# Splitting the weights in the first woven period of a delta-rule attention and MLP kernel: the remainder on VectorE, loads on other queues, the last unit woven in

## The chip, the cores and the metric

The kernel runs on one core of one Trainium2 chip. The metric is the device time of one execution in microseconds; for the kernel before it is the median of three runs. Where a single execution is taken apart, it is the profiled one, with its own time.

## The reference

q, k and v have 4 batches, 8 heads, 768 steps and 48 elements a head, in float32. Each head carries a 48 x 48 state; step by step the output is the state read with q, and the state is then corrected by the delta rule:

```python
k_n = k / (np.linalg.norm(k, axis=-1, keepdims=True) + 1e-06)
for t in range(S):
    y[:, :, t] = np.einsum('bhd,bhde->bhe', q[:, :, t], state)
    v_old = np.einsum('bhde,bhd->bhe', state, kt)
    state = state + bt[:, :, :, None] * np.einsum('bhd,bhe->bhde', kt, vt - v_old)
h = np.maximum(x @ w_in, 0.0)        # x: y as 3072 tokens x 384
return (h * h @ w_out).astype(np.float32)
```

w_in is 384 x 2048 and w_out 2048 x 384, both float64.

## The kernel before, in words

The work is cut into 12 units: two batches and 128 steps each, in two chunks of 64 steps. For a unit the kernel normalizes the keys (`normalize`), forms the products of keys with keys and queries (`static`), inverts a triangular matrix of every 32 steps by substitution on VectorE (`invert`, two instructions a step, L386 to L389), completes the inverse of 64 steps on TensorE (`whole`), carries the state through the two chunks (`sequential`) and runs the two MLP layers on its 256 tokens (`moe`). TensorE takes every float32 operand of the MLP as a high and a low half in fp32r and sums three products (L534, L547).

The weights come as float64. `fetch` loads them as pairs of 32-bit words on SP's queue in 28 pieces (three of w_in with 512 columns, then four of w_out with 384, and so on). `split_weights` turns each piece into its halves: an absolute value on ScalarE (L142), a maximum on GpSimd (L143, `least`), four instructions on VectorE that put the float32 together and form the rest below it (L150 to L157, `words`), the cast to the high half on ScalarE (L160), and on TensorE identity x float32, minus identity x high half and identity x rest, summed in PSUM and copied by ScalarE as the low half (L166, L167, `low`). The high half is written to the place from which the words were read.

The order on TensorE, VectorE, ScalarE and SP is that in which the program emits the instructions; GpSimd's is not written by hand. First come the loads of units 0 and 1 and a fixed sequence with seven pieces (0 to 6), then the inversion of units 0 and 1 together, then pieces 7 to 17 beside unit 0's state. From unit 1 on, `weave` mixes the steps of several generators: each has a number of steps and a stretch of the period, and the steps are sorted by their place. The last generator (the MLP of the unit before) is the filler: between two steps of other generators that are not marked "quiet" one of its steps is put. Pieces 18 to 27 stand in the period of unit 1, as 11 steps.

```python
        for u in range(1, units):
            parts = [(splits, NS, 0, 0.88, "")] if u == 1 else []
            ...
            parts.append((before, n_moe - OVER, M0, M1, ""))
            weave(*parts)
        take(before)
        take(moe(ds_[units - 1]))
```

## Time and profile before

| what | value |
|---|---|
| median of 3 runs | 703.48 us (701.7 to 704.35) |
| profiled execution, its own time | 702.14 us |
| its span, first to last instruction | 700.2 us |
| TensorE busy | 631.6 us, 90% |
| VectorE busy | 429.3 us, 61% |
| ScalarE busy | 332.2 us, 47% |
| GpSimd busy | 85.0 us, 12% |
| mean granted TensorE clock | 0.976 of full speed |

PE is TensorE's matmul, PEld its weight loads, DVE VectorE, ACT ScalarE, POOL GpSimd, SP SyncE. A timeline row gives start, duration, engine, line, operation, output<-input, the count, and in brackets the idle time of the engine before it with what ended it. A busy share over the whole span is an average over stages with different limits: here an opening in which TensorE has little to do, and eleven woven periods in which it has little rest.

### The profile page before, as it was taken

How to read it: one execution, taken by the hardware profiler on the slowest of the kernel's cores; microseconds unless marked ns; L12 is line 12 of the kernel's file. 1: busy time of each engine (PE TensorE's matmuls, PEld its weight loads, DVE VectorE, ACT ScalarE, POOL GpSimd, SP SyncE). 2: the span in 40 equal slices, each digit the busy share in tenths (PEclk: the TensorE clock that was granted, in tenths of full speed). 3: DMA queues.
4: the chain of work that ended last, by engine and by line, in shares of the span. 5: the costliest groups of instructions: out<-in, count | busy, mean ns of one | idle time of the engine just before them, and what ended most of it. 6: DMA issues, size and time to landing. Idle time of an engine off the chain costs nothing.

```text
span 700.2 us, 23645 instructions
## 1 busy us (share of the span) xinstructions
PE 631.6 (90%) x10104; PEld 579.8 (83%) x10104; DVE 429.3 (61%) x1165; ACT 332.2 (47%) x632; POOL 85.0 (12%) x110
## 2 busy tenths in 40 slices
PE   2740598798999999999999999999999999999996
PEld 1420257687999999999999999999999999999996
DVE  3599985568549468477576485593775775641221
ACT  3550366464553553544545535445545445355352
POOL 7970341210100100101001001001000010000000
PEclk9985799999999999999999999999999999999999
DMA  8788331400341441531522423415315324030100
GB/s 171 178 234 335 74 51 17 93 9 2 54 101 25 80 88 19 107 65 28 102 51 43 98 40 54 102 24 107 70 18 103 60 35 98 3 61 3 24 1 23
DMA packets 172969, 49.96 MB, mean 71 GB/s; under 512 B 164513, under 2 KB 167617, under 8 KB 172865
## 3 DMA queue, kind: packets, MB, share of 16 engines
q1 hardware_dynamic: 169920, 47.65, 32.3%
q8 instruction: 79, 1.29, 0.8%
q0 software_dynamic: 768, 0.41, 0.3%
q10 hardware_dynamic: 2176, 0.39, 0.3%
q14 instruction: 26, 0.20, 0.1%
HBM read 37.32 MB, written 11.01 MB: 69 GB/s over the span
## 4 chain that ended last, share of the span: by engine, by line
PE 80%; DVE 9%; DMA 3%; ACT 2%; issue 2%; SPq 2%; POOL 1%; DVEq 0%; ACTq 0%
PE h L547 30%; PE o L534 29%; PE g L478 3%; PE g L454 3%; PE x L447 2%; DVE tt L389 2%; PE x L300 2%; PE x L491 2%; DVE h_h L386 2%; DMA w<-in_moe_w_in_dram 1%; PE g L499 1%; PE x L166 1%; PE g L300 1%; SPq L205 1%; PE x L290 1%
## 5 line engine op out<-in xcount | busy, mean ns | idle before, releaser
L534 PE MATMUL o<-w,h_h 128*128 128x384 f32 x768 | 203.7, 346 | 0.0
L547 PE MATMUL h<-x_h,w 128*128 128x256 f32 x1152 | 172.4, 285 | 2.3 <-ACT x_h L516 1.3
L547 PEld LDWEIGHTS h<-x_h,w 128*128 128x128 f32 x1152 | 152.6, 188 | 8.0 <-ACT x_h L516 2.7
L526 DVE TENSOR_TENSOR h_l<-r,h_h 128x512 fp32r<-128x512 f32 x96 | 66.5, 692 | 147.6 <-PE o L534 59.3
L554 ACT ACTIVATE r<-h 128x512 f32<-128x512 f32 x96 | 57.4, 598 | 172.9 <-PE h L547 172.5
L534 PEld LDWEIGHTS o<-w,h_h 128*128 128x128 f32 x768 | 133.5, 189 | 2.5
L534 PE MATMUL o<-w,h_l 128*128 128x384 f32 x384 | 130.0, 338 | 0.0
L388 DVE SCALAR_TENSOR_TENSOR tmp<-lt,bt,z 128x126 f32<-128x126 f32 (+22 forms) x310 | 95.5, 308 | 21.4 <-DMA out_dram<-a 10.4
L547 PE MATMUL h<-x_l,w 128*128 128x256 f32 x576 | 99.2, 281 | 0.0
L389 DVE TENSOR_TENSOR z<-z,tmp 128x126 f32<-128x126 f32 (+22 forms) x310 | 79.2, 255 | 10.6
L547 PEld LDWEIGHTS h<-x_l,w 128*128 128x128 f32 x576 | 81.4, 188 | 0.0
L534 PEld LDWEIGHTS o<-w,h_l 128*128 128x128 f32 x384 | 72.3, 188 | 0.0
L555 ACT ACTIVATE r<-r 128x512 f32<-128x512 f32 x96 | 60.7, 632 | 3.1
L557 ACT CAST h_h<-r 128x512 fp32r<-128x512 f32 x96 | 59.5, 620 | 3.0
L372 POOL MEMSET z<- 128x512 f32 x10 | 5.5, 553 | 395.7 <-DMA inv<-z 348.8
L166 PE MATMUL o<-r,plus 128*128 128x512 f32 (+1 forms) x16 | 8.8, 637 | 28.3 <-DVE r L153 28.3
L247 DVE TENSOR_REDUCE n<-rest 128x8 f32<-128x384 f32 x22 | 11.9, 549 | 35.3 <-ACT rest L246 35.3
L143 POOL TENSOR_SCALAR a<-a 128x384 f32<-128x384 f32 (+1 forms) x18 | 24.1, 1340 | 50.4 <-ACT a L142 42.5
L439 ACT ACTIVATE tt<-x 32x256 f32<-32x256 f32 x42 | 15.7, 375 | 26.6 <-PE x L435 26.1
L166 PEld LDWEIGHTS o<-r,plus 128*128 128x128 f32 x16 | 2.7, 204 | 29.2 <-ACT s L249 28.1
L478 PEld LDWEIGHTS g<-state,kq 48*64 48x64 f32 x1408 | 22.5, 134 | 4.3 <-issue 2.8
L516 ACT CAST x_h<-h 128x384 fp32r<-128x384 f32 x24 | 11.4, 480 | 30.7 <-PE h L514 30.7
(144 smaller groups left out, 801.6 us busy)
## 6 DMA issues: line engine op xcount, KB each, us to landing
w<-in_moe_w_in_dram SPq DMA_DIRECT2D x12, 512.0 KB
w<-in_moe_w_out_dram SPq DMA_DIRECT2D x16, 384.0 KB
lt<-blocks SPq DMA_DIRECT2D x22, 256.0 KB
vt<-in_v_dram SPq DMA_DIRECT2D x96, 48.0 KB
out_dram<-a SPq DMA_DIRECT2D x48, 96.0 KB
kpad<-in_k_dram SPq DMA_DIRECT2D x88, 48.0 KB
qpad<-in_q_dram SPq DMA_DIRECT2D x84, 48.0 KB
blocks<-ap SPq DMA_DIRECT2D x48, 64.0 KB
```

What stands on the lines that cost most here:

```text
L143: nc.gpsimd.tensor_scalar(out=a.bitcast(F32), in0=a.bitcast(F32), scalar1=LEAST, scalar2=None, op0=ALU.max)
L300: nc.tensor.matmul(ps[j][b * C:(b + 1) * C, p], lhsT=kq[rows, c, p, b, 0], rhs=kq[rows, c, p, b, first:first + n].rearrange("p x t -> p (x ...
L388: nc.vector.scalar_tensor_tensor(out=tmp, scalar=bt[:, s:s + 1], op0=ALU.mult, op1=ALU.mult, **factors)
L389: nc.vector.tensor_tensor(out=z[:, :nj, s + 1:], in0=z[:, :nj, s + 1:], in1=tmp, op=ALU.subtract)
L454: nc.tensor.matmul(g[rows, c, h], lhsT=tt[rows, c, h], rhs=vt[rows, c, h], start=True, stop=True)
L478: nc.tensor.matmul(dst[to * C:(to + 1) * C, j, p], lhsT=kq[rows, c, p, b, x], rhs=s[rows, b, p], start=(x == 0 and p == 0), stop=False, sk ...
L526: nc.vector.tensor_tensor(out=h_l, in0=r, in1=h_h.bitcast(F32), op=ALU.subtract)
L534: nc.tensor.matmul(o[i], lhsT=a[:, e, i * P:(i + 1) * P], rhs=halves["wo", ft][w], start=(ft == 0 and n == 0), stop=(ft == FT - 1 and n == 2))
L547: nc.tensor.matmul(hp[:, e], lhsT=halves["wi", (kt, ft // EACH)][w][:, f], rhs=x[:, kt], start=(n == 0), stop=(n == 3 * KT - 1))
L554: nc.scalar.activation(out=r, in_=hp, func=AF.Relu)
L555: nc.scalar.activation(out=r, in_=r, func=AF.Square)
L557: nc.scalar.copy(out=h_h, in_=r)
```

## The change

High half and remainder: `words` no longer casts; a new step `high` does. In the opening the order stays as it was. In the woven period (`split_early` false) a piece takes three steps instead of one: the remainder of the piece before and the words of this one; the absolute value and maximum of the next; the low half of the piece before and the cast of this one. The remainder float32 - high half is a VectorE subtraction there, and TensorE sums two products, identity x remainder and identity x rest, instead of three. The pieces' steps become quiet ones, 35 by number.

Loads: GpSimd's queue keeps the beta of unit 0 alone; unit 0's q and unit 1's beta go to SP, unit 1's q to SP and later, after the triangles' transfers; two weight loads go ahead of unit 1's keys.

Last unit: the first two steps of its MLP are woven between the last four of the unit before, and two of its four stores are issued by ScalarE.

```diff
@@ -129,7 +129,7 @@
                 raws.append(raw)
 
     def room(x, n):
-        pool, first, second = rooms[x % 2 if x < AHEAD else 0]
+        pool, first, second = rooms[x % 2 if x < AHEAD - 1 else 0]
         return pool.tile([P, PC], I32, name=first)[:, :n], pool.tile([P, PC], I32, name=second)[:, :n]
 
     def split_weights():
@@ -156,33 +156,60 @@
             nc.vector.tensor_scalar(out=w1, in0=a, scalar1=-0x800000, scalar2=None, op0=ALU.bitwise_and)
             nc.vector.scalar_tensor_tensor(out=rest.bitcast(F32R), in0=raw[:, :, 0].bitcast(U32), scalar=2.0 ** -52,
                                            in1=w1.bitcast(F32), op0=ALU.mult, op1=ALU.mult)
-            hl = wpool.tile([P, 2, raw.shape[1]], F32R, name=place[x])
+            return x, a, rest
+
+        def high(x, a, rest):
+            hl = wpool.tile([P, 2, raws[x].shape[1]], F32R, name=place[x])
             nc.scalar.copy(out=hl[:, 0], in_=a.bitcast(F32))
             return x, a, rest, hl
 
-        def low(x, a, rest, hl, bank):
-            ps = bank()[:, :hl.shape[2]]
-            for n, (m, y) in enumerate(((ident, a.bitcast(F32)), (minus, hl[:, 0]), (plus, rest.bitcast(F32R)))):
-                nc.tensor.matmul(ps, lhsT=m, rhs=y, start=(n == 0), stop=(n == 2))
+        def low(x, a, rest, hl, formed=False):
+            ps = split_bank()[:, :hl.shape[2]]
+            first = [(plus, hl[:, 1])] if formed else [(ident, a.bitcast(F32)), (minus, hl[:, 0])]
+            for m, y in first:
+                nc.tensor.matmul(ps, lhsT=m, rhs=y, start=(m is first[0][0]), stop=False)
+            nc.tensor.matmul(ps, lhsT=plus, rhs=rest.bitcast(F32R), start=False, stop=True)
             nc.scalar.copy(out=hl[:, 1], in_=ps)
             halves[weight_parts[x][:2]] = hl[:, 0], hl[:, 1]
 
-        before, ready = None, []
-        for x in range(NW):
+        def remainder(x, a, rest, hl):
+
+            nc.vector.tensor_tensor(out=hl[:, 1], in0=a.bitcast(F32), in1=hl[:, 0].bitcast(F32), op=ALU.subtract)
+
+        before, ready, x = None, [], 0
+        while split_early:
 
             far = 3 if x < AHEAD - 3 else 1
-            while x + len(ready) < min(NW, x + far):
+            while len(ready) < far:
                 ready.append(least(x + len(ready)))
             if x == 0:
                 yield
+            now = high(*words(*ready.pop(0)))
+            if before:
+                low(*before)
+            before = now
+            x += 1
+            while len(ready) < (far if x < AHEAD - 3 else 1):
+                ready.append(least(x + len(ready)))
+            yield
+
+        low(*before)
+        before = None
+        for x in range(x, NW):
+            if before:
+                remainder(*before)
             now = words(*ready.pop(0))
+            yield
+            if not ready and x + 1 < NW:
+                ready.append(least(x + 1))
+            yield
             if before:
-                low(*before, split_bank)
-            before = now
-            while x + 1 + len(ready) < min(NW, x + 1 + (far if x + 1 < AHEAD - 3 else 1)):
-                ready.append(least(x + 1 + len(ready)))
-            yield
-        low(*before, split_bank)
+                low(*before, formed=True)
+            before = high(*now)
+            yield
+        remainder(*before)
+        yield
+        low(*before, formed=True)
         yield
 
     def split_bank():
@@ -214,7 +241,7 @@
     def load_q(d):
 
         d["qp"] = kpad[2] if d["u"] == 1 else qp
-        load_to(d["qp"], q, d, D, (nc.sync, nc.gpsimd) if d["u"] <= 1 else None)
+        load_to(d["qp"], q, d, D)
 
     def load_beta(d):
 
@@ -223,7 +250,7 @@
         t0, b0, x = d["t0"], d["b0"], C * (d["u"] == 1)
 
         by = beta[b0:b0 + 2, :, t0:t0 + P].rearrange("b h (c n s) -> b n c h s", n=2, s=HB)
-        queue = nc.gpsimd if first else nc.sync
+        queue = nc.gpsimd if d["u"] == 0 else nc.sync
         for n in range(4):
             for j in range(2):
                 queue.dma_start(out=d["bt"][x + n * H2 + j:x + (n + 1) * H2:2], in_=by[n // 2 ^ j, n % 2][:, j::2])
@@ -241,7 +268,7 @@
         for c in range(NC):
             h = slice(c * H, (c + 1) * H)
 
-            sq = (apool.tile([P, H, D], F32, name="r", bufs=2) if d["u"] == 2 else
+            sq = (apool.tile([P, H, D], F32, name="r", bufs=2) if d["u"] in (2, 3) else
                   spool.tile([P, PC], F32, name="rest")[:, :H * D].rearrange("p (h e) -> p h e", h=H))
             nc.scalar.activation(out=sq, in_=kn[:, h], func=AF.Square)
             nc.vector.tensor_reduce(out=n2[:, h], in_=sq, axis=AX.X, op=ALU.add)
@@ -284,7 +311,7 @@
 
         def transposed(c, which, bank=None):
 
-            src = (d["kp"], d["qp"])[which]
+            src = d["qp" if which else "kp"]
             tp = (x_tile(u) if bank is None else bank).rearrange("p (n t) -> p n t", n=NP)
             for p in range(NP):
                 nc.tensor.transpose(tp[:, p], src[:, c, 2 * p:2 * p + 2].rearrange("p a b -> p (a b)"), ident)
@@ -563,7 +590,7 @@
                 yield from second(fp - 2)
         for fp in (FT // 2 - 2, FT // 2 - 1):
             yield from second(fp)
-        results = []
+        results, last = [], d["u"] == units - 1
         for c in range(2):
             results.append(spool.tile([P, PC], F32, name="a")[:, :DM])
             (nc.vector.tensor_copy if c else nc.scalar.copy)(out=results[c], in_=o[c])
@@ -571,7 +598,8 @@
         for c in range(2):
             for b in range(2):
                 row = (d["b0"] + b) * S + d["t0"] + c * C
-                nc.sync.dma_start(out=out[row:row + C], in_=results[c][b * C:(b + 1) * C])
+                queue = nc.scalar if last and c == 0 else nc.sync
+                queue.dma_start(out=out[row:row + C], in_=results[c][b * C:(b + 1) * C])
 
     def take(gen, n=None):
         while n is None or n > 0:
@@ -622,7 +650,7 @@
         yield from sequential(d)
 
     F0, F1, F2 = 3, 3, 6
-    NS = NW + 1 - (1 + 6 + 4 + 7)
+    NS = 3 * (NW + 1 - (1 + 6 + 4 + 7)) + 2
     OVER, M0, M1, E2 = 3, 0.032, 0.97, 0.13
     L1, N1 = (0.22, 0.42), (0.62, 0.92)
     A1, Q1 = (0.0, 0.22), (0.34, 0.98)
@@ -634,13 +662,14 @@
     splits = split_weights()
     engines = {mybir.EngineType.PE, mybir.EngineType.SP, mybir.EngineType.DVE, mybir.EngineType.Activation}
     with tc.manual_schedule(engines=engines):
-        ds_ += [load(0), load(1)]
-        fetch(F0)
+        ds_.append(load(0))
+        fetch(F0 - 1)
+        ds_.append(load(1))
+        fetch(1)
+        load_beta(ds_[0])
         load_q(ds_[0])
-        load_q(ds_[1])
+        load_beta(ds_[1])
         fetch(F1)
-        load_beta(ds_[0])
-        load_beta(ds_[1])
         take(normalize(ds_[0]))
         take(normalize(ds_[1]))
         take(splits, 1)
@@ -652,8 +681,10 @@
         fetch(1)
         for d in pair:
             take(d, 1)
+        fetch(2)
+        load_q(ds_[1])
+        fetch(F2 - 2)
         load_v(ds_[0])
-        fetch(F2)
         take(splits, 1)
         for d in pair:
 
@@ -681,7 +712,7 @@
         before = inverse = None
         n_i = round((1 - I0) / (I1 - I0) * NI)
         for u in range(1, units):
-            parts = [(splits, NS, 0, 0.88, "")] if u == 1 else []
+            parts = [(splits, NS, 0, 0.88, "quiet")] if u == 1 else []
             if inverse:
                 parts.append((inverse, NI - n_i, 0, I1 - 1, "quiet"))
             getting = loads(u)
@@ -697,8 +728,11 @@
                 parts.append((inverse, n_i, I0, 1, "quiet"))
             parts.append((before, n_moe - OVER, M0, M1, ""))
             weave(*parts)
+
+        final = moe(ds_[units - 1])
+        weave((before, OVER + 1, 0.2, 1, ""), (final, 2, 0, 0.5, ""))
         take(before)
-        take(moe(ds_[units - 1]))
+        take(final)
 
 
 # ---- launch: one core; inputs and outputs as the reference has them ----
```

## Rows read from the trace of the kernel before

**Rows 1.** Chain of waits, 0 to 110 us: start, duration, what.

```profile
22.51 1.49 POOL a L143
...
45.60 1.22 DVE lt L379
```

**Rows 2.** Timeline of GpSimd (POOL), 0 to 190 us.

```profile
4.73 2.70 POOL L205 DMA_DIRECT2D qpad<-in_q_dram  x4
...
17.44 4.99 POOL L229 DMA_DIRECT2D bt<-in_beta_dram  x9 [0.32 <-DMA kpad<-in_q_dram]
```

**Rows 3.** Timeline of ScalarE (ACT), 0 to 190 us.

```profile
10.38 0.52 ACT L246 ACTIVATE rest<-kpad 128x384 f32<-128x384 f32 x1 [0.60 <-DMA kpad<-in_k_dram]
...
13.43 0.66 ACT L142 ACTIVATE a<-w 128x512 f32<-128x512 f32 x1 [1.30 <-DMA w<-in_moe_w_in_dram]
...
18.18 0.66 ACT L142 ACTIVATE a<-w 128x512 f32<-128x512 f32 x1 [1.86 <-DMA w<-in_moe_w_in_dram]
...
23.79 0.38 ACT L333 COPY ap<-x 128x256 f32<-128x256 f32 x1
```

**Rows 4.** Timeline of VectorE (DVE), two stretches, 5 to 185 us.

```profile
24.02 0.84 DVE L150 TENSOR_SCALAR a<-a 128x512 int32<-128x512 int32 x1 [9.38 <-POOL a L143]
...
30.12 1.49 DVE L150 TENSOR_SCALAR a<-a 128x512 int32<-128x512 int32 x1
...
111.55 0.35 DVE L150 TENSOR_SCALAR r<-r 128x384 int32<-128x384 int32 x1
...
112.93 0.56 DVE L157 SCALAR_TENSOR_TENSOR h_l<-w 128x384 fp32r<-128x384 uint32 x1
...
129.25 0.43 DVE L150 TENSOR_SCALAR a<-a 128x512 int32<-128x512 int32 x1 [2.59 <-issue]
...
164.06 0.35 DVE L150 TENSOR_SCALAR a<-a 128x384 int32<-128x384 int32 x1
```

**Rows 5.** Timeline of SP's queue, 0 to 190 us.

```profile
11.95 6.83 SPq L205 DMA_DIRECT2D kpad<-in_q_dram  x4
...
18.82 1.55 SPq L128 DMA_DIRECT2D w<-in_moe_w_out_dram  x3
...
98.79 5.42 SPq L229 DMA_DIRECT2D bt<-in_beta_dram  x8
```

**Rows 6.** Waits of SP's queue, 30 to 62 us: total, times, longest.

```profile
SPq L395 <- DVE tt L391: 12.6, 1, 12.6
```

**Rows 7.** Busy time by engine in one stretch: length, engines, PEclk, DMA share, GB/s.

```profile
111.10:178.57 67.47, 60.78 (x808) 52.56 (x809) 46.65 (x124) 34.68 (x69) 10.28 (x8) 0.97 0.16 31
```

**Rows 8.** Waits of all engines, 104 to 182 us: total, times, longest.

```profile
ACT w L160 <- DVE rest L157: 19.7, 7, 4.5
```

**Rows 9.** TensorE's busy time with line 166 alone, same stretch.

```profile
111.10:178.57 67.47, 14.85 (x40) 0.97 0.16 31
```

**Rows 10.** Timeline of TensorE (PE), 104 to 184 us.

```profile
121.69 0.81 PE L166 MATMUL x<-a,plus 128*128 128x384 f32 x2
...
122.68 0.51 PE L534 MATMUL o<-w,h_h 128*128 128x384 f32 x2
...
140.23 2.01 PE L166 MATMUL x<-a,plus 128*128 128x512 f32 x2 [2.66 <-ACT w L167]
```

**Rows 11.** Groups of VectorE by line, 111.1 to 178.57 us: busy us, mean ns, idle.

```profile
L388 DVE SCALAR_TENSOR_TENSOR tmp<-lt,bt,z 128x126 f32<-128x126 f32 (+21 forms) x29 | 9.0, 311 | 0.6
...
L389 DVE TENSOR_TENSOR z<-z,tmp 128x126 f32<-128x126 f32 (+21 forms) x29 | 7.5, 260 | 1.0
...
L526 DVE TENSOR_TENSOR h_l<-r,h_h 128x512 fp32r<-128x512 f32 x8 | 5.7, 708 | 4.7 <-ACT h_h L557 3.4 <-PE o L534 1.3
```

**Rows 12.** Timeline of all engines, 640 to 702 us.

```profile
658.99 0.82 PE L514 MATMUL h<-plus,y 128*128 128x128 f32 x6
...
660.73 0.94 PE L547 MATMUL h<-x_h,w 128*128 128x256 f32 x6 [0.93 <-DVE x_l L517]
...
694.95 2.39 SPq L574 DMA_DIRECT2D out_dram<-a  x4
```


## The prediction

> **What bounds the kernel now.** I read the page first, then the chain of waits, the timelines of single engines up to 180 us, and the waits and busy times of the first woven period. From about 180 us to the end the chain is TensorE work without gaps, so that part moves only where the change touches its last unit. The time that can move lies before.
>
> *Opening.* The chain goes through GpSimd's first maximum (L143) at 22.51 us and then VectorE to 45.60 us, where the serial inversion of units 0 and 1 (L379 on) begins [rows 1]. The maximum was not late for data: ScalarE had its input ready at 13.43 + 0.66 = 14.09 [rows 3]. GpSimd was still issuing loads, q from 4.73 and beta until 17.44 + 4.99 = 22.43 [rows 2]. So VectorE sat idle for 9.38 us before its first piece at 24.02, and seven pieces of weights then took until 45.60, 3.08 us each [rows 1, 4].
>
> *First woven period (unit 0's MLP with pieces 18 to 27 of the weights).* From its first product at 111.10 to that of the next unit at 178.57 it lasts 67.47 us; TensorE is busy for 60.78 and so idle for 6.69, VectorE is busy for 46.65 [rows 7]. ScalarE stood 19.7 us waiting for VectorE's last word instruction of a piece (L157) [rows 8]: its cast of the high half is next in its queue, and the absolute value of the next piece, which GpSimd's maximum and VectorE's words need, stands behind that cast. The pieces thus run in a ring through three engines: words of piece 22 at 129.25, of piece 27 at 164.06, so 34.81 / 5 = 6.96 us a piece [rows 4], though a piece's words alone take 112.93 + 0.56 - 111.55 = 1.94.
>
> **The change, part by part.**
>
> *Loads off GpSimd.* It loses eight q and eight beta loads and keeps the eight of unit 0's beta. Four loads took 2.70 before the waits began, so eight take 5.4, and it is free at about 4.7 + 5.4 = 10.1 instead of 22.43 [rows 2]. The next gate is ScalarE. Two weight loads now stand ahead of unit 1's keys on SP, at 1.55 / 3 = 0.52 each [rows 5]: the keys land 1.0 us later if only the issue counts, 3 if the transfer ahead counts too. I take 1.5, so the last square of unit 1 starts at 11.9 instead of 10.38. The first absolute value followed it by 13.43 - 10.38 = 3.05, 1.30 of that waiting for weights, which now come sooner: 11.9 + 1.75 = 13.6. Three of 0.66 end at 15.6, and the last product copy (L333), which ended at 24.17, 5.33 after the third (18.84), now ends near 21 [rows 3]. SP then has four more q loads than now for unit 0 (4 x 0.68, eight beta loads costing 5.42, so 2.7) and eight beta loads (5.4), and loses unit 1's four q loads with their waits (6.83): weights 3 to 5 are issued at 18.82 + 2.7 + 5.4 - 6.83 = 20.1 at the earliest, and I let them land at 24 [rows 5]. From there: absolute value 0.6, maximum 1.4, words 2.2, then three more pieces at the 3.1 that rows 4 show, while ScalarE and GpSimd also serve the products of q: 24 + 4.2 + 9.3 = 37.5. The inversion begins there instead of 45.60: 8.1 us. Ends: 11 if the 24 is 21; 3 if the keys or the weights land 5 us later than taken.
>
> Unit 1's q moves behind the transfers of the triangles. Its transposes stand in ScalarE's queue behind the absolute values of pieces 3 to 6, so the seven pieces ahead of the inversion don't need it; its lateness is covered by the inversion itself. SP's later loads slip by the eight issues added there less what it saves earlier, 2 to 3 us; SP now waits 12.6 us for the end of the inversion [rows 6], so with 8.1 less and 3 more it still has 1.5. If that cover goes, the inverse waits behind the last weights, 1 to 3 us. I take 8.
>
> *High half cast a piece later, remainder on VectorE, two products.* On TensorE, ten pieces used 14.85 us in the period [rows 9]. A 384-column piece takes 122.68 - 121.69 = 0.99 for four instructions, 0.81 of it the two against the identity, overlapping the rest [rows 10]. Bounds for the two products that remain: 0.99 - 0.81 = 0.18 and half, 0.50. I take 0.4, since the remaining two are the short ones: 4 us for ten, and TensorE's need falls to 60.78 - 14.85 + 4 = 49.9. VectorE gains ten subtractions of the form of L526, 0.708 each [rows 11]: at most 7.1, so it needs 53.7 where TensorE needs 49.9. VectorE becomes the bound of this period. Its load per piece in the second half: words 2.0 to 2.4, remainder 0.6, three and a bit steps of the next inversion at 0.311 + 0.260 (1.9), half an h_l (0.4), and small work of normalization and state (0.4): 5.5 us in place of 6.96. Over the five spacings that is 1.46 x 5 = 7.3. In the first half TensorE saves 0.6 on each of four pieces, but the new wait (VectorE's remainder for ScalarE's cast, with the next words, the masks of the next unit and the h_l subtractions queued behind it, for which TensorE waits) can eat this; I take nothing. So 7 for the period. The ends: 13.8 if VectorE runs without a gap (67.47 - 53.7), and a loss of 7.1 if the additions come on top of the present ring.
>
> VectorE's words took longer while GpSimd worked: one first instruction of a piece took 1.49 us at 30.12, against 0.35 at 111.55 [rows 4]. In this period the sum uses the undisturbed durations, since GpSimd has only one maximum a piece there. The Trainium skill (SBUF — State Buffer, section "Who interferes with whom") says that a VectorE instruction with two SBUF inputs contends with a GpSimd instruction that reads SBUF, which speaks against putting the remainder there; the 1.49 us agrees, and what it would make of the time is the third rival.
>
> *Last unit woven in.* Before, TensorE ends the unit before at 658.99, transposes for 0.82 and has its next product at 660.73 [rows 12]. Woven, only the transposes remain: 1.74 - 0.82 = 0.9 saved, at best 1.7. The four last stores take 2.39 us of SP's time; split between two queues, two remain behind the later copy, so about 0.6. Together 1.5 (0.5 to 2.3).
>
> The other rooms for piece 19 and for unit 3's squares, and the test for q's tile, cost nothing: the first instructions of that kind run while VectorE sets the pace.
>
> Sum: 8 + 7 + 1.5 = 16.5. The profiled execution took 702.14 (span 700.2, the rest lies around it); the median, 703.48, is 1.34 longer. 703.48 - 16.5 = 687.
>
> **The rivals.**
>
> *1. The opening gives nothing*: 703.48 - 8.5 = 695. SP takes over what GpSimd did, and the weights or keys come later by as much. For it: SP's loads already wait for earlier ones to land (four loads in 6.83 us). GpSimd's order is not written by hand either, so its maxima could stay behind. Against it: the issue alone held GpSimd until 22.43 with data ready at 14.09. The Trainium skill (DMA: Bandwidth & Descriptors, section "Issuing engines are not separate DMA queues") says that starting transfers from several engines only saves the sequencer's time to initiate them, usually small beside the transfer. By that rule this is the case; the trace disagrees with its "small", 17.7 us of GpSimd's queue.
>
> *2. The first woven period gives nothing*: 703.48 - 9.5 = 694. The remainder's wait for the cast replaces the cast's wait for the words. Against it: the next absolute value no longer stands behind that wait.
>
> *3. VectorE and GpSimd collide in the woven period*: each of ten pieces loses 1.49 - 0.35 = 1.1 us, 11 in all, 703.48 - 16.5 + 11 = 698.
>
> *4. Slower.* TensorE waits for a remainder at every piece, long enough to lose its clock. At 140.23, after 2.66 us of idling, one piece of 512 columns took 2.01 us for its first two instructions, where 0.81 for 384 columns makes 1.08, and the mean granted clock of the period is 0.97 [rows 7, 10]: part of it went at the lower of the two levels, 1.2 GHz. With 2.7 of wait and, by the same ratio on 1.5 of products, 1.4 of slow work on each of ten pieces the period lasts 49.9 + 41 = 91, 23.5 more than now: 703.48 + 23.5 - 9.5 = 717. It decides from about eight such pieces; below that the opening outweighs it. Against it: VectorE's load per piece is less than the spacing now.
>
> **How the numbers follow.** Forecast 0.60; rival 1 0.13, rival 2 0.10, rival 3 0.05, rival 4 0.07; 0.05 that rivals 1 and 2 come together, within 0.5% of before, which is about what a measurement of this kernel can tell from no change (700.0 to 707.0). Faster 0.88, same 0.05, slower 0.07. The forecast's own range is 680 (opening 11, period 11, end 2) to 692; rivals 1 and 2 are taken in up to 696.
>
> **What would show it.** Right: GpSimd's first maximum before 17 us; the inversion's start (L379) at 35 to 40; a woven period of 58 to 62 us with VectorE above 85% busy and little waiting of ScalarE for L157; no gap of TensorE at the last unit's start. Wrong: the inversion's start near 45, or VectorE idle before remainders, or the granted clock of the period under 0.95.

## The result, and the profile after

The changed kernel took 693.97 us (median of 4 runs, 691.14 to 696.97) beside 703.25 for the kernel before on the same chip: a ratio of 0.987, 95% interval 0.9824 to 0.9916. Measured once more later it took 695.12 (5 runs, 693.5 to 696.98) beside 701.89: 0.9911 (0.9897 to 0.9925). It is faster by 7 to 9 us; the forecast was 16.5, to 687.

| stretch, profiled executions | before | after | difference | predicted |
|---|---|---|---|---|
| start to the first product of the woven period | 111.10 | 109.28 | -1.82 | -8 |
| first woven period | 67.47 | 62.73 | -4.74 | -7 |
| its end to the last unit's first product | 482.16 | 480.88 | -1.28 | -0.9 |
| last unit | 39.47 | 38.91 | -0.56 | -0.6 |
| span | 700.2 | 691.8 | -8.4 | -16.5 |

**The opening began as forecast.** The timeline of GpSimd after has its first maximum at 15.84 where rows 1 have 22.51:

```profile
15.84 1.49 POOL L143 TENSOR_SCALAR a<-a 128x512 f32<-128x512 f32 x1 [1.70 <-ACT a L142]
```

The timeline of VectorE after has its first piece at 17.96 (24.02 in [rows 4]) and the inversion of units 0 and 1 (now L406) at 38.55, 7.05 sooner than the 45.60 of [rows 1]. Its last step ends at 66.57:

```profile
17.96 0.83 DVE L150 TENSOR_SCALAR a<-a 128x512 int32<-128x512 int32 x1
...
38.55 1.22 DVE L406 TENSOR_TENSOR lt<-lt,bt 128x1024 f32<-128x1024 f32 x1
...
65.34 1.23 DVE L418 TENSOR_TENSOR tt<-tt,bt 128x1024 f32<-128x1024 f32 x1
```

**Then the gain stops at the inverse's transfers.** The inversion's result goes out to memory (`inv<-tt`) and comes back rearranged (`tt<-inv`) before TensorE can go on. SP's timeline, first before, then after:

```profile
72.61 1.15 SPq L395 DMA_DIRECT2D inv<-tt  x2
75.72 1.93 SPq L404 DMA_DIRECT2D tt<-inv  x4
```

```profile
63.71 3.26 SPq L128 DMA_DIRECT2D w<-in_moe_w_out_dram  x4
67.69 1.70 SPq L422 DMA_DIRECT2D inv<-tt  x2
76.04 1.93 SPq L431 DMA_DIRECT2D tt<-inv  x4
```

The inverse is sent 4.92 us sooner and read back 0.32 later. The waits of SP's queue after, 60 to 80 us (total, times, longest), say what it stood for, the landing of the inverse itself; before, the same wait was 1.9 us:

```profile
SPq L431 <- DMA inv<-tt: 6.6, 1, 6.6
```

Busy time by engine after, in stretches of 5 us (columns as in [rows 7]), shows why, and what came of it:

```profile
65.00:70.00 5.00, 1.31 (x2) 0.50 (x2) 4.72 (x11) 0.38 (x2) 0.00 (x0) 0.50 1.03 417
70.00:75.00 5.00, 4.98 (x9) 1.97 (x8) 4.55 (x13) 2.87 (x6) 0.00 (x0) 0.54 1.03 398
75.00:80.00 5.00, 1.78 (x34) 0.67 (x36) 2.80 (x5) 1.55 (x3) 3.27 (x4) 1.00 0.52 109
80.00:85.00 5.00, 4.64 (x129) 2.83 (x114) 3.84 (x9) 2.48 (x6) 2.20 (x2) 0.64 0.53 84
85.00:90.00 5.00, 4.95 (x89) 4.08 (x90) 4.50 (x9) 4.61 (x11) 2.91 (x2) 0.50 0.38 66
90.00:95.00 5.00, 5.00 (x99) 4.16 (x100) 1.21 (x3) 2.87 (x7) 0.77 (x2) 0.83 0.37 65
```

From 65 to 75 us the last two numbers of a row (DMA share, GB/s) are 1.03 and about 400: the transfers are full with the last weights, and the inverse lies behind them. From 75 to 80 TensorE (first pair) works 1.78 of 5 us, and the granted clock (third from the end) then falls to 0.64, 0.50, 0.83; before, it was 1.00 in all three of the stretches from 80 on. TensorE's timeline after has the waits:

```profile
78.68 0.22 PE L454 MATMUL x<-tt,ap 32*32 32x32 f32 x2 [1.74 <-DMA tt<-inv]
79.76 0.74 PE L454 MATMUL x<-tt,ap 32*32 32x32 f32 x62 [0.86 <-DMA tt<-inv]
```

**The woven period** after (columns as in [rows 7]) has TensorE 5.36 us less busy and VectorE 6.30 more, 84% of the period:

```profile
109.28:172.01 62.73, 55.42 (x788) 50.88 (x789) 52.95 (x134) 35.20 (x68) 11.10 (x8) 0.95 0.17 33
```

The waits after, 109 to 172 us: the cast's wait for the words is 2.3 where [rows 8] has 19.7, and TensorE now waits 5.7 for the new remainder (L177).

```profile
PE x L170 <- DVE w L177: 5.7, 7, 2.8
...
DVE w L177 <- ACT w L163: 2.5, 2, 2.1
ACT w L163 <- DVE rest L157: 2.3, 4, 1.2
```

**The last unit.** TensorE's timeline after: the unit before ends, and the next product starts at once, where [rows 12] have 0.82 of transposes and 0.93 of idling:

```profile
652.71 0.34 PE L561 MATMUL o<-w,h_l 128*128 128x384 f32 x1
652.89 0.87 PE L574 MATMUL h<-x_h,w 128*128 128x256 f32 x6
```

### The profile page after: what moved, and what is told of

It reads as the page before. It is cut to its first block, busy times and chain, and to the rows that moved or that the text cites. A ratio compares the mean times of both kernels' runs of the same rounds, so it can differ in the third digit from the quotient of the medians.

```text
span 691.8 us, 23593 instructions
## 1 busy us (share of the span) xinstructions
PE 628.9 (91%) x10084; PEld 583.2 (84%) x10084; DVE 433.1 (63%) x1175; ACT 332.8 (48%) x632; POOL 76.4 (11%) x94
## 4 chain that ended last, share of the span: by engine, by line
PE 78%; DVE 4%; ACT 1%; issue 1%; DVEq 0%
PE h L574 30%; PE o L561 29%; PE g L505 3%; PE g L481 3%; PE x L518 2%; PE x L474 2%; PE x L327 2%; PE g L526 1%; PE g L327 1%; PE g L317 1%; PE x L317 1%; PE h L541 1%; PE x L462 1%; PE x L454 1%; DVE tmp L415 1%
## 5 line engine op out<-in xcount | busy, mean ns | idle before, releaser
L143 POOL TENSOR_SCALAR a<-a 128x384 f32<-128x384 f32 (+1 forms) x19 | 26.6, 1399 | 47.0 <-ACT a L142 46.8
L170 PE MATMUL o<-r,plus 128*128 128x512 f32 (+1 forms) x16 | 10.4, 737 | 19.8 <-DVE r L153 19.8
L481 PE MATMUL g<-vt,tt 64*64 64x48 f32 x768 | 25.8, 223 | 0.0
```

Of the source, the lines that this page charges most:

```text
L143: nc.gpsimd.tensor_scalar(out=a.bitcast(F32), in0=a.bitcast(F32), scalar1=LEAST, scalar2=None, op0=ALU.max)
L481: nc.tensor.matmul(g[rows, c, h], lhsT=tt[rows, c, h], rhs=vt[rows, c, h], start=True, stop=True)
```

## The experiments

Theory from the profiles above: the opening's gain stands behind the last weights' bytes, and the woven period gains by the remainder and the two products. All runs are timed against the kernel before on the same chip. "Start" is the first product of the woven period and "period" its length, in the profiled execution.

| kernel | median us | ratio to before, interval | start | period |
|---|---|---|---|---|
| before | 703.48 | | 111.10 | 67.47 |
| changed | 693.97 | 0.987 (0.9824 to 0.9916) | 109.28 | 62.73 |
| changed, again | 695.12 | 0.9911 (0.9897 to 0.9925) | 109.10 | 62.81 |
| loads alone | 702.09 | 0.9993 (0.9974 to 1.0012) | 110.52 | 68.78 |
| split alone | 696.5 | 0.9917 (0.9896 to 0.9938) | 110.16 | 62.77 |
| last unit alone | 700.8 | 0.9981 (0.9969 to 0.9993) | 110.55 | 68.42 |
| weights right after the inverse | 693.47 | 0.9867 (0.9846 to 0.9889) | 107.84 | 62.73 |
| unit 1's beta on GpSimd | 690.99 | 0.9851 (0.9822 to 0.9881) | 106.58 | 62.72 |
| three products | 691.68 | 0.9849 (0.9827 to 0.9871) | 107.62 | 62.03 |
| weights after the loads | 689.17 | 0.981 (0.979 to 0.9831) | 105.01 | 62.76 |
| both of these | 689.57 | 0.9822 (0.9807 to 0.9838) | 104.80 | 62.04 |
| cast early, finer turns | 704.88 | 1.0042 (1.0026 to 1.0059) | 110.28 | 73.24 |
| weights after, beta on GpSimd | 688.65 | 0.9813 (0.9799 to 0.9828) | 105.57 | 61.22 |
| cast late, one turn | 694.74 | 0.988 (0.9856 to 0.9905) | 112.41 | 61.47 |

### One part at a time

The kernel before with one of the change's three parts: the order and the queues of the loads; the split in the woven period with its turns and rooms; the last unit's weaving and stores (each as in the diff ahead of the prediction).

> The kernel before with only the loads moved (order of the weight loads, q and beta on other queues). Theory: the inversion starts near 38.6 us and ends near 66.6, but its result's transfer lands near 76, as in the changed kernel, because weights issued late stand ahead of it; the woven period starts 1.8 us earlier than the 111.1 of before, so the time is 703.25 - 1.8 = 701.4. Rival: the opening keeps its gain of 6 us when the rest is unchanged, and is lost only in interplay with the new order of the pieces; then the period starts at 105 and the time is 697.

> The kernel before with only the new treatment of the pieces (high half a piece later, remainder on VectorE, two products, three quiet steps). Theory: the woven period takes 62.7 us instead of 67.5, nothing else moves: 703.25 - 4.7 = 698.5. Rival: the shorter period hangs on the other parts; alone it gains less than 2 us, 701.3 or more.

> The kernel before with only the last unit woven in and two stores issued by ScalarE. Theory: 1.3 us saved before the last unit's first product and 0.6 at the stores: 703.25 - 1.9 = 701.4. Rival: the two steps cost as much where they now stand, and the time stays within 0.5 us of 703.25.

The loads alone give nothing that can be measured, the split 5.8 us by the ratio (0.0083 x 702.4), the last unit 1.3 (0.0019 x 702.4). As ratios to 703.25 the theories' numbers lie within the intervals of their runs. The loads alone do bring the first maximum to 15.92, but SP's timeline of that run has the inverse's reload at 76.86, 1.14 later than before:

```profile
68.54 1.71 SPq L395 DMA_DIRECT2D inv<-tt  x2
76.86 1.92 SPq L404 DMA_DIRECT2D tt<-inv  x4
```

So the 6.59 us won at the first maximum are gone by then; the woven period's new steps have no part in that loss.

### What holds the inverse: bytes, issue time, or the work

First the last eight weights behind the inverse's transfers:

```diff
-        fetch(NW)
+        fetch(NW - 8 - len(raws))
         take(invert(ds_[0]))
+        fetch(NW)
```

> The changed kernel with the last eight weight loads issued after the inverse's transfers instead of ahead of them. Theory (the opening's gain is spent behind those weights): the inverse lands 4 to 5 us earlier (its reload is issued near 71 instead of 76.0), TensorE does not cool down there, the woven period starts near 105 instead of 109.3, and the time falls by about 4 us, to 690. Rival (GpSimd's memset with the maxima queued behind it, or the slow clock, holds unit 0's state whatever the weights do): the reload may come earlier, but the period still starts at 108 to 110 and the time stays at 693 to 695.

The reload came at 70.01, 6.03 sooner than in the changed kernel, but the start only 1.44 sooner, and the time is the same: the theory fell, and start and time are close to the rival's. TensorE's timeline of this run has a new stop, after which its clock was 0.66 from 90 to 95 us:

```profile
89.53 0.81 PE L170 MATMUL o<-a,plus 128*128 128x384 f32 x2 [1.96 <-DVE rest L157]
```

The row names VectorE's word instruction of 88.68, but that belongs to the next piece: this product's own words had ended at 84.17 and its cast at 85.06 (timelines of VectorE and ScalarE), and in the run with the weights still later, below, the same product starts at 87.89, ahead of that word instruction (89.07). So it was something else. The weights move just then: the DMA view of 85 to 89.5 us of this run counts (packets, MB, share of 16 engines) one packet of the queue called instruction, which I take for a load of an engine's code, beside 487 data packets that take 99.3%:

```profile
q1 hardware_dynamic: 487, 1.63, 99.3%
q8 instruction: 1, 0.02, 1.3%
```

That TensorE waited for this code is my reading of the two together; no run here shows it by itself. Next, the weights still later, after the loads of unit 1's v and unit 2's q and beta; and, as a test of SP's issue time, unit 1's beta on GpSimd's queue with the weights where the change has them:

```diff
-        fetch(NW)
+        fetch(NW - 8 - len(raws))
...
         load_beta(ds_[2])
+        fetch(NW)
```

```diff
-        queue = nc.gpsimd if d["u"] == 0 else nc.sync
+        queue = nc.gpsimd if first else nc.sync
```

> The changed kernel with its last eight weight loads issued not before the inverse's transfers (67.69, 76.04) but after the loads of unit 1's v and unit 2's q and beta, at about 98 to 104 us. Theory A, the weights' bytes hold first the inverse (in the changed kernel) and then what comes right behind it (a load of TensorE's code and unit 1's v, where the weights follow the inverse directly): the reload is issued at 70, the state's products end by 87.5, TensorE has no wait of 2 us at 87.6, and the period with the weights starts at 104 to 106 us instead of 109.28; the run is 689 to 691 us. Theory B, what stands still after the inverse is bound by VectorE's and ScalarE's splits and not by transfers: the period starts at 107.5 to 108.5 us as with the weights right behind the inverse, 692.5 to 693.5 us. Rival: the weights now come late for the woven period (first words of the piece that waits for them after 112 us): 695 us or more.

> The changed kernel, with the eight loads of unit 1's beta on GpSimd's queue again: 5.40 us less on SP's queue ahead of the weights (issue row 16.29), 4.5 us more on GpSimd's queue ahead of the first maximum (now at 15.84, so it comes at about 17.3, and the inversion starts up to 1.5 us later). Theory A, SP's issue time is what holds the inverse: the last weights are issued 4 to 5 us sooner, the inverse's two transfers at about 66.5 and 71 instead of 67.69 and 76.04, the period with the weights starts 3 to 4 us sooner, 690 us. Theory B, the bytes are what holds it (about 400 GB/s while the inverse's transfer waits): the weights move into a stretch where the engines of the DMA are half idle, so the reload comes 2 to 3 us sooner, but what is won is partly lost to the later first maximum and to a new wait behind it: 692 to 694 us. Rival, neither (each weight waits for an earlier one to land): 694 to 695 us.

With the weights after the loads the start is 105.01 and the time 689.17, inside the first theory's numbers. SP's timeline of that run:

```profile
66.85 1.15 SPq L422 DMA_DIRECT2D inv<-tt  x2
71.05 1.93 SPq L431 DMA_DIRECT2D tt<-inv  x4
```

Busy time in stretches of 5 us in that run: TensorE works 3.36, 3.55 and 5.00 us, and the clock is 1.00 in all three, where the changed kernel has 1.00, 0.64 and 0.50.

```profile
75.00:80.00 5.00, 3.36 (x70) 1.53 (x70) 4.62 (x10) 2.02 (x5) 2.20 (x2) 1.00 0.44 70
80.00:85.00 5.00, 3.55 (x80) 2.18 (x80) 4.50 (x9) 4.13 (x12) 2.63 (x2) 1.00 0.32 53
85.00:90.00 5.00, 5.00 (x130) 4.24 (x130) 4.28 (x8) 4.47 (x9) 1.72 (x2) 1.00 0.40 66
```

TensorE's timelines, first here and then in the changed kernel, part what was won. The products of the inverse (L454) end at 78.57 here and at 80.50 there (79.76 + 0.74, above); the products of the state (L481) follow:

```profile
77.82 0.75 PE L454 MATMUL x<-tt,ap 32*32 32x32 f32 x64
...
85.94 2.02 PE L481 MATMUL g<-vt,tt 64*64 64x48 f32 x62
```

```profile
88.95 3.26 PE L481 MATMUL g<-vt,tt 64*64 64x48 f32 x62
```

The reload is 4.99 us sooner, the end of the inverse's products only 1.93, because TensorE stood at other products until 77.82. The state's products end 4.25 sooner (87.96 for 92.21), and from there both take the same 17.1 us to the start. Of the 4.27 us, 1.93 is thus the inverse, and 2.32 the stretch behind it, where the same 62 products took 3.26 us instead of 2.02.

Beta on GpSimd came out between its first two theories in the median (690.99), in a wide spread (688.32 to 695.09), and its reload was only 0.58 sooner (75.46) with an inversion that began 1.33 later (39.88). TensorE's products of the inverse ended at 80.31, about as in the changed kernel (80.50), and the clock from 85 to 90 us was 0.94 instead of 0.50. What it saved in this execution thus lies behind the inverse and not in the chain up to it. The last two runs of this group put the edits together, and the changed kernel beside them:

> The changed kernel with the last eight weight loads behind the loads of unit 1's v and unit 2's q and beta, and unit 1's beta on GpSimd's queue as well. Theory A, what unit 1's beta on SP cost was only that the weights behind it came later to the inverse's transfers; with the last eight weights out of their way there is nothing left to win, and the first maximum comes some 1.5 us later: 689 to 690 us, no better than 689.17 with the weights moved alone. Theory B, SP's issue time is a cost of its own: another 2 to 3 us, 686 to 687 us.

> The changed kernel as it is, beside the version with the weights moved on the same chip. If moving the weights is a gain of its own: 693 to 694 us here against 689 to 690 there, with intervals that don't overlap. Rival, the 4.5 us between them came from the chip or from the clock after the waits at 78 to 80 us: this kernel too is at 690 to 691 us.

688.65 against 695.12 on one chip, with intervals far apart: the two edits together are worth 6.5 us. Beta on GpSimd adds nothing that can be told once the weights are out of the way (0.9813 and 0.981), so the gain is that of moving the weights, and SP's issue time is no cost of its own. By the ratios of the weights moved alone it is 4 us against the first measurement of the changed kernel and 7 against the second.

### What gives the woven period its 5 us

The changed kernel with three TensorE products again and no remainder on VectorE; its turns and the late cast stay:

```diff
-            if before:
-                remainder(*before)
             now = words(*ready.pop(0))
...
             if before:
-                low(*before, formed=True)
+                low(*before)
             before = high(*now)
...
-        remainder(*before)
         yield
-        low(*before, formed=True)
+        low(*before)
```

> The changed kernel with its new order of steps, but in the woven period the low half again by three TensorE products, with no remainder on VectorE. Removes from VectorE 10 remainders at 593 ns, 5.9 us; adds to TensorE about 1.1 us for each of 10 pieces, 11 us. Theory A, the two products are what gives (TensorE's sum bounds the period): busy time of TensorE goes from 55.4 to about 66 us, the period from 62.7 to 68 to 70 us, the run is 699 to 701 us. Theory B, the later place of the high halves' cast alone gives most of the 4.7 us, because it takes away the waits for it: the period stays under 65 us, 694 to 696 us.

The theory that I held, the first, fell, and the time came out below the second's too. Busy time of this run in its period (62.03 us) and of the changed kernel's [above, 62.73]:

```profile
107.62:169.65 62.03, 59.44 (x809) 53.25 (x809) 47.18 (x124) 34.42 (x69) 10.31 (x8) 0.97 0.19 34
```

TensorE works 59.44 us, about as much as before [rows 7], VectorE 47.18, and the period is as short as with two products. TensorE waits for no remainder; its 4 us more of work take the place of 5.7 us of waits. The groups of the changed kernel's period by line (busy us, mean ns, idle before) show both sides of that exchange: 7.9 us of products for the ten pieces (14.5 with three: 10.99 on the first line and 3.54 on the second), 5.7 of idling before them, and 5.9 of new work on VectorE.

```profile
L170 PE MATMUL x<-w,plus 128*128 128x384 f32 (+1 forms) x10 | 4.4, 435 | 5.7 <-DVE w L177 5.7
L171 PE MATMUL x<-rest,plus 128*128 128x384 f32 (+1 forms) x10 | 3.5, 353 | 0.0
```

```profile
L177 DVE TENSOR_TENSOR w<-a,w 128x384 fp32r<-128x384 f32 (+1 forms) x10 | 5.9, 593 | 2.6 <-ACT w L163 2.5
```

What is left of the change there is the cast's place and the finer turns. Two runs part them, both with three products; their edits are shown against the run above. In the first the cast goes back behind the words, in three turns; in the second it stays late, in one turn a piece as before:

```diff
-            now = words(*ready.pop(0))
+            now = high(*words(*ready.pop(0)))
...
-            before = high(*now)
+            before = now
```

```diff
             now = words(*ready.pop(0))
-            yield
             if not ready and x + 1 < NW:
                 ready.append(least(x + 1))
-            yield
...
-    NS = 3 * (NW + 1 - (1 + 6 + 4 + 7)) + 2
+    NS = NW + 1 - (1 + 6 + 4 + 7)
...
-            parts = [(splits, NS, 0, 0.88, "quiet")] if u == 1 else []
+            parts = [(splits, NS, 0, 0.88, "")] if u == 1 else []
```

> The kernel with three products and no remainder, but the high half's cast put back right behind the four VectorE steps of its own piece, in the same turn; the products stay where they are, two turns later. It tells the place of the cast from the finer turns (three to a piece instead of one). Theory A, the cast's place gives the 5 us: ScalarE waits again for VectorE's last step at each piece (19.7 us in the kernel before), its queue with the MoE's activations behind it, and the period goes from 62.0 to 66 or 67 us: 695 to 697 us. Theory B, the finer turns and the products' distance from the cast give it: ScalarE's waits come back in part, but TensorE no longer stands behind the cast that it needs at once; the period stays at 62 to 63.5 us: 690 to 693 us.

> The kernel with three products and no remainder, with the late cast (behind the next piece's absolute value and the low half of the piece before), but one turn for a piece, followed by a step of the MLP, as in the kernel before. With the run whose cast stands early in finer turns (period 73.2 us) it makes the two parts of the new order complete. Theory A, it is the cast's place in ScalarE's queue alone: the next piece's absolute value and maximum no longer stand behind it, and the period is 62 to 64 us: 691 to 693 us. Theory B, the cast must also be a turn later in time, since in one turn ScalarE still reaches it while VectorE forms the words (1.9 us) and its queue stands there with the MLP's activations behind: waits for L157 of 10 to 20 us, period 65 to 68 us: 695 to 698 us.

Busy time in the period, first with the cast early in finer turns, then with the cast late in one turn:

```profile
110.28:183.52 73.24, 64.05 (x809) 56.23 (x809) 47.12 (x124) 34.61 (x68) 10.28 (x8) 0.93 0.15 29
```

```profile
112.41:173.88 61.47, 58.20 (x808) 51.74 (x809) 47.53 (x124) 34.79 (x69) 10.37 (x8) 1.00 0.18 34
```

Three products in all four cases:

| | one turn a piece | three turns a piece |
|---|---|---|
| cast right behind the words | 67.47 (before) | 73.24 |
| cast behind the next absolute value and the low half | 61.47 | 62.03 |

The cast's place gives 6.0 us in one turn and 11.2 in three; the finer turns by themselves lose. With the early cast and finer turns the period is longer than either theory had it; with the late cast in one turn it is shorter than both. In three turns the cast alone moves; in one turn ScalarE's order of cast, low half and next absolute value is turned round, so there the step is not the cast's alone. Each period is one execution, and with the old split it was 68.78 and 68.42 in two other runs. TensorE had the same products in all four cases (67.47, 73.24, 61.47 and 62.03 us long): it was busy for 60.78, 64.05, 58.20 and 59.44 us at a granted clock of 0.97, 0.93, 1.00 and 0.97, and idle for 6.69, 9.19, 3.27 and 2.59. So part of the 6.0 and of the 11.2 us is the clock; that the clock follows from the waits is likely, but no run shows it by itself. The waits of the two runs, in the same order, add how:

```profile
ACT w L163 <- DVE rest L157: 22.3, 9, 4.0
```

```profile
ACT w L163 <- DVE rest L157: 12.1, 5, 4.2
```

With one turn and the late cast ScalarE still stands 12.1 us for the words, against 19.7 before [rows 8], but at a place where nothing that a piece needs is behind it: the next piece's absolute value has been issued. So it is not this wait alone that cost the 6 us, but what was queued behind it. Its median (694.74) is no better than the changed kernel's. In its profiled execution (695.81) the period started at 112.41: TensorE waited 2.99 + 0.57 us for the inverse, and the clock was 0.50 from 85 to 95 us.

```profile
80.58 0.21 PE L448 MATMUL x<-tt,ap 32*32 32x32 f32 x2 [2.99 <-DMA tt<-inv]
```

The opening of this run, of the three products (start 107.62) and of the changed kernel (109.28) is one program. Their starts differ by 4.8 us: the first product of the inverse came 1.19 us later here than with three products (80.58 and 79.39), and the rest went in the products behind it. TensorE's timelines have the same 62 products of the state, first here and then with three products:

```profile
91.89 3.47 PE L475 MATMUL g<-vt,tt 64*64 64x48 f32 x62
```

```profile
88.54 2.02 PE L478 MATMUL g<-vt,tt 64*64 64x48 f32 x62
```

Last, the two edits that had not lost:

> Both edits that did not lose, together: the last eight weight loads behind the loads of unit 1's v and unit 2's q and beta, and in the woven period three TensorE products and no remainder on VectorE. Theory A, they lie in different stretches and add: the period with the weights starts at 105 us (105.01 with the weights moved alone) and takes 62.0 us (62.03 with three products alone, against 62.73), with no wait of TensorE for the remainder: 688 to 689 us, 0 to 1 us under the kernel with the weights moved alone (689.17). Theory B, the 690 to 692 of the three products was a better clock in the stretch 85 to 95 us (1.00 granted, against 0.50 and 0.83 in the changed kernel), which the moved weights bring by themselves, and the period's 0.7 us is within what runs differ by: 689 to 690 us. Rival: with TensorE at 59.4 of 62.0 us busy, the late weights now make it wait: over 691 us.

689.57, the same as with the weights moved alone: the second theory. The period is 0.7 us shorter with three products (62.04 and 62.76), but it was 61.22 with two in the run with beta on GpSimd, so two and three products can't be told apart here. The best versions are the three with the weights moved, at 688.65 to 689.57, some 13 us under the kernel before.

## Why the prediction was right, and where it was wrong

It held the time (693.97 and 695.12, between 680 and 696) and the direction. But the forecast of 687 was not met, nor the forecast's own range of 680 to 692: the time lies inside because the range was drawn out to 696 for rivals 1 and 2, and that is in part luck. One of its two large terms failed, and the other was in part right for a reason that fell.

**Opening, 8 predicted, 1.82 measured.** The steps up to the inversion held: GpSimd's first maximum before 17 us, the inversion's start at 38.55 for 37.5. The step that failed is "SP's later loads slip by the eight issues added there less what it saves earlier, 2 to 3 us; SP now waits 12.6 us for the end of the inversion, so with 8.1 less and 3 more it still has 1.5". The cover was counted in SP's issue time, and in that it nearly held: the inversion ended at 66.57 and the inverse was sent at 67.69, 1.1 us late where 1.5 were to be left. But the last weights, issued from 63.71 on, had yet to be moved. By the sizes in the profile the eight that the experiment moved are 5 x 384 + 3 x 512 = 3456 KB, some 8.8 us at the 400 GB/s of that stretch. The cover ended with their landing, not their issue, and the wait for the inverse's landing went from 1.9 to 6.6 us. The sentence behind it, "If that cover goes, the inverse waits behind the last weights, 1 to 3 us", named the right wait, but the wait grew by 4.7, and what follows was left out: TensorE idles for 2.6 us and then works partly at the lower clock, which the sum looked for in the woven period alone. With the weights out of the way the term was 6.09 (111.10 to 105.01).

So rival 1 (695, the opening gives nothing), at a chance of 0.13, came nearest for this part. Its number alone would not tell: rival 2 gives 694, and the 695 counts 0 for the opening and 7 for the period, where 1.82 and 4.74 came. Its reason, weights or keys that come later, was wrong for the start and right for the end of the opening: the last four weights were issued from 63.71 on instead of 56.68. The Trainium skill (DMA: Bandwidth & Descriptors, section "Issuing engines are not separate DMA queues"), which the prediction weighed there, says that starting transfers from several engines saves only the time to initiate them. The prediction set GpSimd's 17.7 us of queue against its "usually small". In the run with the loads moved alone the time to initiate was not small, 6.59 us at the first maximum, and none of it was left in the result, a ratio of 0.9993.

**Woven period, 7 predicted, 4.74 measured.** The place was right and the cover was right: ScalarE's wait for L157 fell from 19.7 to 2.3; a period of 58 to 62 us with VectorE above 85% was asked, 62.73 with 84% came. The mechanism was only half right. The step that failed is the sum "TensorE's need falls to 49.9 [...] VectorE becomes the bound of this period" as the price of the remainder and the two products: with three products and no remainder the period is as short. TensorE's busy time fell by 5.36 only (60.78 to 55.42) where 10.9 was reckoned: the two products of a piece took 0.79 us and not 0.4, 7.9 for ten, and the other work of the period 1.6 longer (55.42 - 7.9 = 47.5 for 60.78 - 14.85 = 45.9), at a mean clock of 0.95 instead of 0.97. What carried the term is the other sentence, on the ring through three engines that the cast closes [rows 4, 8]; opening it was worth 6 us without the remainder and the two products.

**Last unit, 1.5 predicted.** 1.84 in the profiles (1.28 + 0.56), 1.3 by the ratio of that part alone. The gap of TensorE is gone, and two stores less stand at the end. Right.

**Rivals 2 to 4.** The woven period gave most of the gain, so rival 2 fell. For rival 3, the remainder took 593 ns on average (555 at 384 columns; the 708 taken for it is for 512), and the words did not stretch by 1.1 us a piece: their four instructions took 2.12 us on average, 1.99 before. The prediction read its 1.49 us wrongly in two ways. The 0.35 beside it is for 384 columns, and 512 took 0.43 at 129.25 [rows 4]; and the instruction has one input, so it does not bear out a rule on two. A stretch of an instruction with two inputs came elsewhere: at 45.68 in the inversion one took 0.68 us between neighbours of 0.37 and 0.39, while GpSimd worked from 45.46 to 46.99; the neighbour of 0.39 lay beside GpSimd's work too. Rival 4's clock came, but in the opening: the period's own was 0.95, just at the bound named, and TensorE's waits for remainders were 5.7 us in all, not 2.7 at each piece.

## What to carry to other kernels

When a step before a transfer becomes faster, ask which bytes are still moving when the transfer is issued, not only which queue is free; here 3456 KB of weights, the first of them read only at 110.36, left 1.82 us of the opening's gain, and 6.09 when they were issued later. When an engine's queue waits, look at what stands behind the waiting instruction: a cast put behind its neighbours instead of ahead of them was worth 6 us (clock included), and the rewrite around it nothing that could be told. A short stop of TensorE can cost more than its length where the clock falls after it (here 1.93 us at the inverse's products and 2.32 more behind them), so a transfer that it waits for can be worth more than the wait in the table.

## What the runs showed of the hardware

After 2.6 us of waiting for the inverse, the granted clock of the changed kernel was 0.64, 0.50 and 0.83 of full speed in the next three stretches of 5 us, though TensorE was busy for 4.64 to 5.00 of each. In another execution of the same opening, after 2.39 us of waiting (three products), it was 0.66, 1.00 and 1.00; in the second execution of the changed kernel, after only 1.40 us, 0.58, 0.50 and 0.89. So the length of this wait does not order the clock behind it. With the weights moved and three products there was no wait for the inverse, and one stretch (80 to 85 us) still had 0.66, but the period started as early as in the other runs with the weights moved (104.80). A value of 0.50 is the lower of the two levels, 1.2 of 2.4 GHz. How long the clock stayed there differed from run to run, and with the 1.19 us of the later inverse it moved the period's start from 107.62 to 112.41, though the program up to there was the same. The three versions with the weights behind the loads also spread less, 1.6 to 2.6 us from the lowest to the highest time, where the changed kernel has 5.8 and 3.5; that is 4 or 5 runs each, and that the clock is the reason is not shown.
